# Attention row sums moved into the weighted sums' PSUM bank, with two weighted-sum turns per head instead of three

## The chip, the cores and the metric

The kernel runs on one core of a Trainium2 chip. The metric is the device time in microseconds (us) of one execution; the kernel before takes 891.99 us, the median of three runs from 890.58 to 896.3.

## The reference, cut to what matters

Four batches of eight heads, 1152 keys, 64 dimensions. Neighbouring queries are averaged, so 576 query rows remain per head. The attention output goes through a two-layer network with a parametric ReLU.

```
q_pool = q.reshape(B, H, S // 2, 2, D).mean(axis=3)
scores = scale * (q_pool @ k.T)
attn = exp(scores - max(scores))
attn = attn / (sum(attn) + 1e-09)
x = (attn @ v) laid out as tokens x 512            # 2304 x 512
h = x @ w_in                                       # 512 -> 2048
y = (max(h, 0) + alpha * min(h, 0)) @ w_out        # 2048 -> 512
```

## The kernel before, in words

**Tiling.** A head's scores are computed transposed: nine chunks `c` of 128 keys on the partitions, 576 queries on the free axis in two halves `h` of `HQ` = 288. For each chunk and half two matmuls (L884, L885) fill one of three `s` banks, ScalarE takes the exponential into tile `p` (L897), and `p` (128x2x288) then serves two sums over the keys. The weighted sums `av` = v^T p are matmuls of 64 columns of weights, half 0 into partitions 0-63 and half 1 into 64-127 (L925); the one `av` bank holds 288 of its 512 fp32 columns. The row sums are made in two steps: adds on VectorE (DVE) and GpSimd (POOL) fold three `p` tiles into one partial sum `acc` (L913), and for a pair of heads 12 matmuls with a 128x32 block of ones (L947) sum the partitions of the six partial sums, into an `s` bank, four 32-column groups side by side. ScalarE copies the sums out with eps (L959), a DMA chain through memory turns them for the reciprocal and broadcasts it, and `av` is scaled by it (L984). Matrices of fp32 (not the rounded fp32r) run as two recorded instructions each: 1152 for L925 and 384 for L947.

**Turns.** The scores use the whole 128x128 array, the two sums use it in 64-column or 32-column groups. A run of matmuls in column groups between full-width ones is called a turn here. Before, `G=3` makes three turns of three chunks per head (`weighted`), and one further turn per pair of heads for the row sums (`sums` in `pair_end`).

**Order.** The order of every engine's instructions is worked out by a list scheduler when the kernel is built (`Scheduler`): each task has an engine, a duration, a priority and the buffers it takes, and each engine's queue is in that order on the chip. `prio` is the head's number plus a fraction; `col=True` marks the tasks in column groups and `col_cost` keeps them together. Rings limit the buffers in flight: `PB` for `p`, `AB` for `acc`, one `av` bank.

**Stages.** Up to about 200 us the `m` banks (for the row maxima, L816, reduced by DVE in L833) and three `s` banks hold PSUM, and DVE also converts the first weights. After head 9 (`SWITCH=9`) the banks are dealt anew, one `m` bank pair less, two `h` banks more, and the network's lower part for finished batches (`low_sweep`, L401) fills what TensorE has left. From about 537 us on only the network runs (`low_sweep` of the rest, then `high_sweep`).

Of the kernel before, what the change touches and what calls it, by code (L numbers as in the profile page):

```python
# [182 lines left out]
def attention_ffn(  # L183
# [9 lines left out]
    PB: int = 8,  # L193
# [61 lines left out]
    HQ = SQ // 2  # L255
    NQT = (SQ + P - 1) // P
# [262 lines left out]
    r_rs = Ring([P, HQ], F32, "rs", 1)  # L519
# [13 lines left out]
    s_tasks, acc, avs = {}, {}, {}  # L533
# [338 lines left out]
    def head_main(n, k1, q1, vv):  # L872
        acc[n], avs[n] = [], Buf(r_avs)
        av = Buf(r_av)
        p0, t_acc, t_av, ps_ = None, None, None, []
        for c in range(NC):
# [25 lines left out]
            J = JS[n >= JH]  # L902
            if c % J == 0:

                p0, t_acc = p, None
                part = Buf(r_acc)
                acc[n].append(part)
            else:
                a, b = (p0, p) if c % J == 1 else (part, p)
                eng, dur, e = (DVE, dve(2 * HQ), nc.vector) if c in ADDS[n >= JH] else (POOL, 2.4 * 2 * HQ + 50, nc.gpsimd)  # L910
                t_acc = add(
                    eng, dur,
                    lambda a=a, b=b, part=part, e=e: e.tensor_tensor(out=part.t, in0=a.t, in1=b.t, op=ALU.add),  # L913
                    reads=[a, b], writes=[part], deps=[t_acc] if t_acc else [], prio=n + c / NC, lock=True,
                )

            ps_.append(p)
            if len(ps_) < G and c < NC - 1:
                continue

            def weighted(c=c, ps_=ps_):
                for i, p in enumerate(ps_):
                    e = c - len(ps_) + 1 + i
                    for h in (1, 0):
# [5 lines left out]
            t_av = add(  # L930
                PE, 552 * len(ps_), weighted, reads=[vv] + ps_, writes=[av], deps=[t_av] if t_av else [],
                prio=n + (c + GL) / NC, col=True,
            )
            ps_ = []
# [3 lines left out]
        )  # L938

    def pair_end(n):  # L940
        ps, rs, rsd, rc, rrd = Buf(r_ps), Buf(r_rs), Buf(r_rsd), Buf(r_rc), Buf(r_rrd)

        def sums():
            J = JS[n >= JH]
            for j in range(NC // J):
                for g in (3, 2, 1, 0):
                    nc.tensor.matmul(  # L947
                        out=ps.t[g * 32:(g + 1) * 32, :HQ], lhsT=ones, rhs=acc[n + g // 2][j].t[:, g % 2],
                        start=j == 0, stop=j == NC // J - 1, tile_position=(0, g * 32),
                    )  # L950

        def flat(d):
# [3 lines left out]
        add(PE, 500 * NC // JS[n >= JH], sums, reads=acc[n] + acc[n + 1], writes=[ps], prio=e, col=True, kind="s")  # L956
        add(
            ACT, act(HQ, True) + 93,
            lambda: nc.scalar.activation(out=rs.t, in_=ps.t[:, :HQ], func=AF.Identity, bias=eps),  # L959
            reads=[ps], writes=[rs], prio=e,  # L960
        )
        add(SP, 600, lambda: nc.sync.dma_start(out=rsd.t, in_=rs.t[0:P:32]), reads=[rs], writes=[rsd], prio=e)
# [201 lines left out]
```

## Time and profile before

| | |
|---|---|
| median of three runs | 891.99 us |
| the three runs | 890.58, 891.99, 896.3 us |
| span of the profiled execution, first to last instruction | 894.6 us |
| TensorE busy | 98% of the span |
| DVE, ScalarE, POOL busy | 70%, 58%, 19% |

The profiled execution is another one than the three runs; what lies around its span isn't recorded, and its span lies inside the range of the three. A matmul's recorded duration includes the time it takes to drain, so neighbouring records overlap: what a matmul costs is read from the distance between two starts.

### The profile page before, as it was taken

To read this page: it belongs to the slowest core of one execution; us is meant where nothing else is said; L and a number is where in the kernel's file an instruction comes from. 1 tells how busy PE (TensorE), PEld (TensorE's weight loads), DVE (VectorE), ACT (ScalarE), POOL (GpSimd) and SP (SyncE) were. 2 spreads that over 40 slices of the span, in tenths; PEclk is the share of its full clock that TensorE was granted. 3 is DMA by queue.
4 is the path that set the end of the run, shared out by engine and by line. 5 is a ranking of instruction groups with operands and counts; after the bars stand their busy time and mean duration, and the time that the engine had idled before them with its cause. 6 is when DMAs were issued, how large, how long until landed. Compare 5 with 4: busy or idle time off the path is not lost.

```text
span 894.6 us, 16888 instructions
## 1 busy us (share of the span) xinstructions
PE 874.9 (98%) x6273; PEld 742.6 (83%) x6273; DVE 622.8 (70%) x984; ACT 514.5 (58%) x1337; POOL 171.3 (19%) x126
## 2 busy tenths in 40 slices
PE   8799899999999999999999999999999999999998
PEld 5577666767777787777777779999999999999998
DVE  5899999987877778887798993478953243243332
ACT  4667767676776667766676664466543243333432
POOL 3323322323333323333322320000000000000000
PEclk9999999999999999999999999999999999999999
DMA  8756687677655855954745334955333113112000
GB/s 258 167 146 164 159 209 193 160 206 178 163 123 161 195 158 107 226 127 126 176 107 134 88 101 136 320 176 173 118 106 107 54 54 107 53 54 93 1 27 27
DMA packets 59496, 121.71 MB, mean 136 GB/s; under 512 B 12795, under 2 KB 25622, under 8 KB 59414
## 3 DMA queue, kind: packets, MB, share of 16 engines
q1 hardware_dynamic: 57254, 111.79, 43.8%
q0 software_dynamic: 2160, 8.85, 5.7%
q8 instruction: 49, 0.80, 0.4%
q14 instruction: 33, 0.27, 0.1%
HBM read 92.36 MB, written 19.02 MB: 124 GB/s over the span
## 4 chain that ended last, share of the span: by engine, by line
PE 82%; DVE 12%; ACT 3%; issue 2%; DMA 1%; POOL 0%; DVEq 0%; ACTq 0%; POOLq 0%
PE h L401 30%; PE y L401 16%; PE av L925 12%; PE s L884 7%; PE m L816 7%; PE s L885 6%; DVE bx L833 4%; PE s L947 2%; DVE acc L913 2%; PE av L1048 1%; ACT p L897 1%; PE m L797 1%; DVE q L632 1%; DVE k L619 1%; DVE mm L858 1%
## 5 line engine op out<-in xcount | busy, mean ns | idle before, releaser
L897 ACT ACTIVATE p<-s 128x288 f32<-128x288 f32 x576 | 205.0, 409 | 81.1 <-PE s L885 76.7
L913 POOL TENSOR_TENSOR acc<-acc,p 128x576 f32<-128x576 f32 x96 | 151.1, 1574 | 352.3 <-ACT p L897 159.1
L833 DVE TENSOR_REDUCE bx<-m 128x2 f32<-128x768 f32 x192 | 179.8, 949 | 40.8 <-PE m L816 39.5
L884 PE MATMUL s<-q,k 128*128 128x288 f32 x576 | 171.6, 312 | 1.0 <-ACT p L897 0.8
L885 PE MATMUL s<-q,k 65*128 65x288 f32 x576 | 165.4, 300 | 0.0
L925 PE MATMUL av<-p,vv 128*64 128x288 f32 x1152 | 161.7, 416 | 0.0
L429 DVE SCALAR_TENSOR_TENSOR pos<-neg,nal,pos 128x288 f32<-128x288 f32 x128 | 67.0, 526 | 106.8 <-ACT neg L423 101.9
L884 PEld LDWEIGHTS s<-q,k 128*128 128x128 f32 x576 | 110.4, 192 | 22.4 <-issue 12.0
L418 ACT ACTIVATE pos<-h 128x288 f32<-128x288 f32 x128 | 51.7, 404 | 120.3 <-PE h L401 120.0
L925 PEld LDWEIGHTS av<-p,vv 128*64 128x64 f32 x1152 | 74.5, 137 | 55.6 <-issue 16.7
L401 PE MATMUL h<-x,wh 128*128 128x288 f32 x576 | 117.8, 297 | 0.0
L816 PE MATMUL m<-k,q 128*128 128x384 f32 (+1 forms) x384 | 107.8, 368 | 6.5 <-DVE q L632 3.9
L885 PEld LDWEIGHTS s<-q,k 65*128 65x128 f32 x576 | 110.7, 192 | 0.1
L401 PE MATMUL y<-gs,wh 128*128 128x288 f32 x512 | 103.0, 295 | 0.0
L401 PEld LDWEIGHTS h<-x,wh 128*128 128x128 f32 x576 | 92.4, 188 | 2.9 <-issue 2.7
L435 ACT ACTIVATE gs<-pos 128x288 fp32r<-128x288 f32 x128 | 56.7, 444 | 60.8 <-DVE pos L429 60.3
L440 DVE TENSOR_TENSOR gs<-pos,gs 128x288 fp32r<-128x288 f32 x128 | 59.1, 464 | 45.5 <-ACT gs L435 45.1
L816 PEld LDWEIGHTS m<-k,q 128*128 128x128 f32 (+1 forms) x384 | 63.2, 198 | 27.7 <-issue 11.8
L401 PE MATMUL h<-x,wl 128*128 128x288 f32 x288 | 84.8, 294 | 0.0
L401 PEld LDWEIGHTS y<-gs,wh 128*128 128x128 f32 x512 | 82.1, 188 | 0.0
L913 DVE TENSOR_TENSOR acc<-p 128x576 f32<-128x576 f32 x96 | 72.4, 755 | 10.8 <-ACT p L897 9.6
L401 PE MATMUL y<-gs,wl 128*128 128x288 f32 x256 | 75.4, 294 | 0.0
(97 smaller groups left out, 1269.4 us busy)
## 6 DMA issues: line engine op xcount, KB each, us to landing
kk<-kt SPq DMA_DIRECT2D x63, 288.0 KB
wraw<-wt SPq DMA_DIRECT2D x32, 512.0 KB
x<-xs SPq DMA_DIRECT2D x48, 288.0 KB
qs<-qt SPq DMA_DIRECT2D x16, 576.0 KB
vv<-vt SPq DMA_DIRECT2D x32, 288.0 KB
xs<-x SPq DMA_DIRECT2D x64, 144.0 KB
k<-k SPq DMA_DIRECT2D x62, 144.0 KB
qs<-qt POOLq DMA_DIRECT2D x15, 576.0 KB, 7.0
```

The lines of the kernel that those rows point to most:

```text
L401: nc.tensor.matmul(out=ps[:, :HQ], lhsT=w[a, c // DMO][:, c % DMO:c % DMO + P], rhs=lo(hl), start=(first and i == 0), stop=(last and i == 2),)
L418: ACT, act(HQ, True), lambda: nc.scalar.activation(out=pos.t, in_=ps.t[:, :HQ], func=AF.Relu),
L429: lambda: nc.vector.scalar_tensor_tensor(out=pos.t, in0=neg.t, scalar=nal[:, f:f + 1], in1=ps.t[:, :HQ] if NT else pos.t, op0=ALU.mult, op ...
L435: ACT, act(HQ), lambda: nc.scalar.activation(out=gs.t[:, 0], in_=pos.t, func=AF.Copy),
L440: lambda: nc.vector.tensor_tensor(out=gs.t[:, 1], in0=pos.t, in1=gs.t[:, 0].bitcast(F32), op=ALU.subtract),
L816: nc.tensor.matmul(out=ms.t[:, i, :JW], lhsT=q1.t[d, PAD + t * P:PAD + (t + 1) * P], rhs=k1.t[d, j * JW:(j + 1) * JW], start=True, stop=True,)
L833: lambda c=c, e=e, step=step, m=len(pair), ms=ms: nc.vector.tensor_reduce(out=bx.t.rearrange("p t j -> p (t j)")[:, c:e + 1:step], in_=ms. ...
L884: nc.tensor.matmul(out=ps.t[:, :HQ], lhsT=k1.t[:, s], rhs=q1.t[:, q], start=True, stop=False)
L885: nc.tensor.matmul(out=ps.t[:, :HQ], lhsT=k2[n % 2][:, s], rhs=q2[n % 2][:, PAD + q.start:PAD + q.stop], start=False, stop=True)
L897: lambda ps=ps, p=p, h=h: nc.scalar.activation(out=p.t[:, h], in_=ps.t[:, :HQ], func=AF.Exp, scale=SCALE),
L913: lambda a=a, b=b, part=part, e=e: e.tensor_tensor(out=part.t, in0=a.t, in1=b.t, op=ALU.add),
L925: nc.tensor.matmul(out=av.t[h * D:(h + 1) * D, :HQ], lhsT=vv.t[:, e], rhs=p.t[:, h], start=(e == 0), stop=(e == NC - 1),)
```

## The change

Weighted sums come in two turns per head, chunks 0-3 and 4-8 (`GROUPS`). Partial sums come from `PARTS`: heads 0-11 have four (chunks 0-3, 4-6, 7, 8; the last two are the `p` tiles themselves), heads 12-31 have three (0-4, 5-7, 8). Adds per head: five (DVE 1 and 5, POOL 2, 3 and 6) or six (DVE 1, 6 and 7, POOL 2, 3 and 4), before six (DVE 1, 4, 7, POOL 2, 5, 8). Each partial sum, seen as 576 columns, is cut into four quarters of `SW` = 144, and four matmuls with the block of ones put their sums into columns 288-431 of the `av` bank (`total`), with a priority right behind the second group. `pair_end` no longer has a turn of its own; ScalarE copies the sums per head, and two DMAs instead of one bring a pair's sums to memory. `PB` goes from 8 to 11, `AB` from 7 to 4, and the `rs` ring from one tile of 288 columns to two of 144.

```
-    PB: int = 8,
+    PB: int = 11,
...
-    G: int = 3,
-    JS: tuple = (3, 9),
-    JH: int = 32,
-    AB: int = 7,
-    ADDS: tuple = ((1, 4, 7), (1, 4, 7)),
+    GROUPS: tuple = (3, 8),
+    PARTS: tuple = (((0, 1, 2, 3), (4, 5, 6), (7,), (8,)), ((0, 1, 2, 3, 4), (5, 6, 7), (8,))),
+    JH: int = 12,
+    AB: int = 4,
+    ADDS: tuple = ((1, 5), (1, 6, 7)),
...
+    SW = SQ // 4
...
-    r_rs = Ring([P, HQ], F32, "rs", 1)
+    r_rs = Ring([P, SW], F32, "rs", 2)
...
+            if c in heads:
+
+                part, first, t_acc = p, True, None
             else:
...
+                a, part = part, Buf(r_acc) if first else part
...
-            if len(ps_) < G and c < NC - 1:
-                continue
...
+            if c in GROUPS:
...
+                t_av.append(add(
+                    PE, 552 * len(ps_), weighted, reads=[vv] + ps_, writes=[av], deps=t_av[-1:],
+                    prio=n + (c + GL) / NC, col=True,
+                ))
+                ps_ = []
+            if c in tails:
+
+                def total(part=part):
+                    q = part.t.rearrange("p h q -> p (h q)")
+                    for g in (3, 2, 1, 0):
                         nc.tensor.matmul(
-                            out=av.t[h * D:(h + 1) * D, :HQ], lhsT=vv.t[:, e], rhs=p.t[:, h],
-                            start=(e == 0), stop=(e == NC - 1),
+                            out=av.t[g * 32:(g + 1) * 32, HQ:HQ + SW], lhsT=ones, rhs=q[:, g * SW:(g + 1) * SW],
+                            start=False, stop=True, tile_position=(0, g * 32), skip_group_check=True,
                         )
...
+                totals.append((total, part, n + (max(c, GROUPS[1]) + GL) / NC + 0.001))
+        for total, part, p in totals:
+            add(PE, 245, total, reads=[part], writes=[av], deps=t_av[:1], prio=p, col=True)
...
+        add(
+            ACT, act(SW, True) + 93,
+            lambda: nc.scalar.activation(out=sums[n].t, in_=av.t[:, HQ:HQ + SW], func=AF.Identity, bias=eps),
+            reads=[av], writes=[sums[n]], prio=n + 1,
+        )
...
-        def sums():
-            J = JS[n >= JH]
-            for j in range(NC // J):
-                for g in (3, 2, 1, 0):
-                    nc.tensor.matmul(
-                        out=ps.t[g * 32:(g + 1) * 32, :HQ], lhsT=ones, rhs=acc[n + g // 2][j].t[:, g % 2],
-                        start=j == 0, stop=j == NC // J - 1, tile_position=(0, g * 32),
-                    )
...
-        add(PE, 500 * NC // JS[n >= JH], sums, reads=acc[n] + acc[n + 1], writes=[ps], prio=e, col=True, kind="s")
...
-        add(SP, 600, lambda: nc.sync.dma_start(out=rsd.t, in_=rs.t[0:P:32]), reads=[rs], writes=[rsd], prio=e)
+        for i in range(2):
+            add(
+                SP, 600,
+                lambda i=i: nc.sync.dma_start(
+                    out=rsd.t[2 * i:2 * i + 2].rearrange("g q -> (g q)").rearrange("(a b) -> a b", b=SW),
+                    in_=sums[n + i].t[0:P:32],
+                ),
+                reads=[sums[n + i]], writes=[rsd], prio=e,
+            )
```

## Rows read from the trace of the kernel before

**Rows 1.** The page: span, and the clock granted to TensorE in 40 slices.
```profile
span 894.6 us, 16888 instructions
...
PEclk9999999999999999999999999999999999999999
```

**Rows 2.** By stage: stretch, length, busy us (xcount) of PE, PEld, DVE, ACT, POOL.
```profile
60.00:200.00 140.00, 134.14 (x925) 94.58 (x925) 134.16 (x196) 102.82 (x266) 44.33 (x32) 0.99 0.72 187
200.00:537.00 337.00, 335.29 (x2459) 258.54 (x2457) 278.36 (x390) 230.20 (x611) 107.70 (x71) 1.00 0.57 144
537.00:895.00 358.00, 353.72 (x2671) 353.25 (x2667) 165.77 (x338) 148.57 (x386) 0.00 (x0) 1.00 0.31 100
```

**Rows 3.** The chain that ended last, 60-200 us: shares of that stretch by line.
```profile
by line: DVE bx L833 16.1%; DVE acc L913 8.2%; PE av L925 7.4%; issue 7.4%; PE s L884 5.8%; ACT p L897 5.3%; PE m L816 4.7%; PE s L885 4.2%; ACT k L605 3.7%; DVE k L619 3.4%; DMA q<-mm 3.3%; DVE wmag L359 3.2%; DVE q L632 3.1%; DVE wl L323 
```

**Rows 4.** Waits in 200-537 us, weight loads, then DVE: total us, times, longest us.
```profile
PEld m L816 <- DVE bx L833: 4.3, 6, 1.3
...
DVE bx L833 <- PE m L816: 32.4, 45, 1.7
```

**Rows 5.** Timeline of TensorE around one weighted turn: start us, us, line.
```profile
201.56 0.30 PE L884 MATMUL s<-q,k 128*128 128x288 f32 x1
201.69 0.30 PE L885 MATMUL s<-q,k 65*128 65x288 f32 x1
201.92 1.68 PE L925 MATMUL av<-p,vv 128*64 128x288 f32 x12
203.53 0.40 PE L884 MATMUL s<-q,k 128*128 128x288 f32 x1
203.76 0.29 PE L885 MATMUL s<-q,k 65*128 65x288 f32 x1
```

**Rows 6.** Timeline of TensorE in four 10 ns stretches inside turns: start us, us.
```profile
202.46 0.41 PE L925 MATMUL av<-p,vv 128*64 128x288 f32 x2
...
203.19 0.41 PE L925 MATMUL av<-p,vv 128*64 128x288 f32 x2
...
212.29 0.43 PE L947 MATMUL s<-acc,ones 128*32 128x288 f32 x4
...
212.53 0.43 PE L947 MATMUL s<-acc,ones 128*32 128x288 f32 x4
```

**Rows 7.** Timeline of TensorE: a turn with weighted sums and row sums joined.
```profile
210.18 1.68 PE L925 MATMUL av<-p,vv 128*64 128x288 f32 x12
211.78 1.66 PE L947 MATMUL s<-acc,ones 128*32 128x288 f32 x24
213.37 0.40 PE L884 MATMUL s<-q,k 128*128 128x288 f32 x1
```

**Rows 8.** Stretches with L925 alone, then those with tile `acc` alone (columns of rows 2).
```profile
28.00:200.00 172.00, 56.08 (x396) 25.82 (x396) 0.97 0.69 176
200.00:537.00 337.00, 105.59 (x756) 48.63 (x756) 1.00 0.57 144
...
28.00:60.00 32.00, 0.00 (x0) 0.00 (x0) 4.40 (x6) 9.22 (x6) 0.89 0.54 126
60.00:200.00 140.00, 8.31 (x120) 3.52 (x120) 20.20 (x27) 40.96 (x28) 0.99 0.72 187
200.00:537.00 337.00, 18.25 (x264) 7.45 (x264) 47.76 (x63) 100.96 (x63) 1.00 0.57 144
```

**Rows 9.** Timeline of TensorE: four matmuls of 384 columns, and the next start.
```profile
204.43 0.87 PE L816 MATMUL m<-k,q 128*128 128x384 f32 x4
205.14 0.30 PE L884 MATMUL s<-q,k 128*128 128x288 f32 x1
```

**Rows 10.** 40 ns with L947 alone: TensorE busy (xcount), weight loads busy (xcount).
```profile
211.77:211.81 0.04, 0.03 (x4) 0.03 (x5) 1.00 0.57 115
```

**Rows 11.** ScalarE groups: busy us, mean ns of one | idle before.
```profile
L853 ACT ACTIVATE mm<-s 5x128 fp32r<-5x128 f32 x31 | 8.1, 262 | 12.8 <-PE s L849 12.7
...
L959 ACT ACTIVATE rs<-s,eps 128x288 f32<-128x288 f32 x16 | 8.0, 499 | 12.7 <-PE s L947 12.7
```

**Rows 12.** Timeline: the last attention output is stored; the first matmul that needs it.
```profile
557.88 2.91 SPq L1006 DMA_DIRECT2D xs<-x  x4
...
579.11 0.29 PE L401 MATMUL h<-x,wh 128*128 128x288 f32 x1
```

More of the change, by code (lines that the diff above doesn't have):

```diff
@@ L532, in attention_ffn @@
     q2_b = [Buf() for n in range(NH)]
-    s_tasks, acc, avs = {}, {}, {}
+    s_tasks, sums, avs = {}, {}, {}
     def old_users(n):
@@ L872, in head_main @@
     def head_main(n, k1, q1, vv):
-        acc[n], avs[n] = [], Buf(r_avs)
+        avs[n], sums[n] = Buf(r_avs), Buf(r_rs)
         av = Buf(r_av)
-        p0, t_acc, t_av, ps_ = None, None, None, []
+        t_acc, t_av, ps_, totals = None, [], [], []
+        late_head = n >= JH
+        heads, tails = [g[0] for g in PARTS[late_head]], [g[-1] for g in PARTS[late_head]]
         for c in range(NC):
@@ L901, in head_main @@
                 )
-            J = JS[n >= JH]
[L903 to L907, printed above, removed]
-            else:
-                a, b = (p0, p) if c % J == 1 else (part, p)
-                eng, dur, e = (DVE, dve(2 * HQ), nc.vector) if c in ADDS[n >= JH] else (POOL, 2.4 * 2 * HQ + 50, nc.gpsimd)
+            if c in heads:
+                part, first, t_acc = p, True, None
+            else:
+                a, part = part, Buf(r_acc) if first else part
+                eng, dur, e = (DVE, dve(2 * HQ), nc.vector) if c in ADDS[late_head] else (POOL, 2.4 * 2 * HQ + 50, nc.gpsimd)
@@ L911, in head_main @@
                 t_acc = add(
                     eng, dur,
-                    lambda a=a, b=b, part=part, e=e: e.tensor_tensor(out=part.t, in0=a.t, in1=b.t, op=ALU.add),
-                    reads=[a, b], writes=[part], deps=[t_acc] if t_acc else [], prio=n + c / NC, lock=True,
+                    lambda a=a, b=p, part=part, e=e: e.tensor_tensor(out=part.t, in0=a.t, in1=b.t, op=ALU.add),
+                    reads=[a, p], writes=[part], deps=[t_acc] if t_acc else [], prio=n + c / NC, lock=True,
@@ L915, in head_main, with weighted @@
                 )
+                first = False
             ps_.append(p)
-            if len(ps_) < G and c < NC - 1:
-                continue
[L921 to L924, printed above, removed]
+            if c in GROUPS:
+                def weighted(c=c, ps_=ps_):
+                    for i, p in enumerate(ps_):
+                        e = c - len(ps_) + 1 + i
+                        for h in (1, 0):
+                            nc.tensor.matmul(
+                                out=av.t[h * D:(h + 1) * D, :HQ], lhsT=vv.t[:, e], rhs=p.t[:, h],
+                                start=(e == 0), stop=(e == NC - 1), skip_group_check=True,
+                            )
[4 more added lines that the diff above has]
+                ps_ = []
@@ L925, in weighted @@
+            if c in tails:
+                def total(part=part):
+                    q = part.t.rearrange("p h q -> p (h q)")
+                    for g in (3, 2, 1, 0):
                         nc.tensor.matmul(
-                            out=av.t[h * D:(h + 1) * D, :HQ], lhsT=vv.t[:, e], rhs=p.t[:, h],
-                            start=(e == 0), stop=(e == NC - 1),
-                        )
-            t_av = add(
-                PE, 552 * len(ps_), weighted, reads=[vv] + ps_, writes=[av], deps=[t_av] if t_av else [],
-                prio=n + (c + GL) / NC, col=True,
-            )
@@ L938, in head_main @@
         )
-    def pair_end(n):
-        ps, rs, rsd, rc, rrd = Buf(r_ps), Buf(r_rs), Buf(r_rsd), Buf(r_rc), Buf(r_rrd)
-        def sums():
-            J = JS[n >= JH]
-            for j in range(NC // J):
-                for g in (3, 2, 1, 0):
-                    nc.tensor.matmul(
-                        out=ps.t[g * 32:(g + 1) * 32, :HQ], lhsT=ones, rhs=acc[n + g // 2][j].t[:, g % 2],
-                        start=j == 0, stop=j == NC // J - 1, tile_position=(0, g * 32),
-                    )
+        add(
[3 more added lines that the diff above has]
+        )
+    def pair_end(n):
+        rsd, rc, rrd = Buf(r_rsd), Buf(r_rc), Buf(r_rrd)
         def flat(d):
@@ L955, in pair_end @@
         e = n + E0
-        add(PE, 500 * NC // JS[n >= JH], sums, reads=acc[n] + acc[n + 1], writes=[ps], prio=e, col=True, kind="s")
[L957 to L961, printed above, removed]
-        add(SP, 600, lambda: nc.sync.dma_start(out=rsd.t, in_=rs.t[0:P:32]), reads=[rs], writes=[rsd], prio=e)
+        for i in range(2):
[6 more added lines that the diff above has]
+                reads=[sums[n + i]], writes=[rsd], prio=e,
+            )
         add(SP, 600, lambda: nc.sync.dma_start(out=rc.t, in_=flat(rsd.t)), reads=[rsd], writes=[rc], prio=e)
```

1 line of the change is left out of this document (removed).

## The prediction

> **What bounds the kernel now.** I read the stages first, then the chain and the waits of each stage, and at last single turns of TensorE. The stages [rows 2]: from 537 us on TensorE is busy 353.72 of 358 us, with nothing of this change in it, so that stretch keeps its length. In 200-537 us TensorE is busy 335.29 of 337 us, while DVE has 278.36 and ScalarE 230.20; the weight loads waited for DVE only 4.3 us in all [rows 4]. There time is TensorE time: what it no longer does is taken over by the network's matmuls that otherwise wait for the stretch after 537 us. In 60-200 us there is no such filler yet, and TensorE (134.14) and DVE (134.16 of 140 us) are both nearly full. The chain there changes engines all the time: DVE's reduce is its largest share, DVE's adds have 8.2%, TensorE's weighted sums 7.4% [rows 3]. So a saving on one engine counts there in part. The granted clock is in its top tenth in every slice [rows 1], the 2.4 GHz level in both stretches (0.99 and 1.00 [rows 2]); the change leaves TensorE no emptier, so I expect nothing of the clock.
>
> **What a turn costs.** Two full-width score matmuls start 0.13 us apart (201.56, 201.69). The weighted turn starts 0.23 after the second, the next full-width matmul starts 1.61 after that, and its follower 0.23 later [rows 5]. Inside the turn a pair (both halves) starts every (203.19 - 202.46) / 3 = 0.243 us [rows 6], so the six pairs of three chunks are 1.46 us of columns, 0.485 per chunk. What is left is the price of the turn: 1.61 - 1.46 = 0.15 inside, 0.10 ahead of it and 0.10 behind it, together 0.35 us. A joined turn lasts 213.37 - 210.18 = 3.19 us [rows 7]; its row sums are six steps of four at 0.24 [rows 6], 1.45 us, so 3.19 - 1.46 - 1.45 - 0.15 = 0.13 us is the change from 64-column to 32-column groups.
>
> **What a new row sum costs.** No row shows four 144-column matmuls in column groups. In the full-width rows the time goes with the columns: 384 of them take (205.14 - 204.43) / 4 = 0.178 us [rows 9] and 288 take 0.13 [rows 5], 1.37 times as long for 1.33 times the columns, so next to nothing is fixed. Halved, a step of four is 0.12 us and a partial sum (two steps) 0.245. The other bound is that the instructions set the pace and not the columns: then a step of four costs what it does now, 0.485 per partial sum. I take 0.245, because four matmuls and five weight loads stand inside 40 ns at the start of a row-sum turn [rows 10], far above the pace that the upper bound needs. A rule speaks against this, in the Trainium skill, TensorE: Matmul & The Clock Gate, Back-to-back issue gap: a stream of weight load and matmul pairs settles at about 81 ns per matmul of 128 columns. By that, eight matmuls are 0.65 us per partial sum and, as an estimate, the whole sum below becomes a loss of 32 us. The trace disagrees: it already runs pairs of 288 columns at 61 ns (four in 0.243 [rows 6]).
>
> **TensorE from 200 us on.** The stretch holds 756 / 12 = 63 weighted turns, which is 21 heads of three, and 264 / 24 = 11 row-sum groups [rows 8]. Two of these follow a weighted turn directly (the one at 210.18 is shown [rows 7]), nine stand alone: 72 turns and two joints. After, 21 heads make 42 turns with 21 joints. Turns: -30 x 0.35 = -10.5 us. Joints: +19 x 0.13 = +2.5. Columns: 11 x 1.45 = 16.0 before; after, 20 heads of three partial sums and one of four, 64 x 0.245 = 15.7: -0.3. Sum -8.3 us. The weighted columns stay.
>
> **TensorE before 200 us.** 396 / 12 = 33 weighted turns and 120 / 24 = 5 row-sum groups, one of them joined: 37 turns. After, 11 heads make 22 turns and 11 joints: -15 x 0.35 + 10 x 0.13 = -4.0 us. Columns: 44 partial sums x 0.245 = 10.8 against 5 x 1.45 = 7.3: +3.5. So TensorE gains only 0.5 us here, and I count it as nothing.
>
> **DVE before 200 us.** 33 adds, three per head, took 4.40 + 20.20 = 24.6 us [rows 8]; 11 go, 8.2 us. How much of it counts: the chain spends 8.2% of 140 us = 11.5 us in these adds [rows 3] out of 20.20 busy, 57%. So -4.7 us. The bounds are 0 (TensorE, busy as long as DVE, ends just as late) and -8.2. The POOL keeps three adds per head, so what DVE loses to it stays.
>
> **What is added.** ScalarE copies 32 sums of 144 columns in place of 16 of 288. A copy of 128 columns took 262 ns and one of 288 with eps 499 [rows 11]; between them, 0.28 to 0.5, I take 0.3: 9.6 us in place of 8.0, beside other work, since ScalarE has 107 us free in 200-537 and 37 in 60-200 [rows 2]. If that cover were gone it would cost 1.6 us, at the upper bound 8. The copy holds the single `av` bank 0.3 us longer; the next user is the next head's first turn, whose priority stands four chunks later, so nobody waits. The copy of the weighted sums now also waits for the row sums behind them, 3 x 0.245 + 0.13 = 0.9 us, with the same cover. The `s` bank that a pair's row sums took, and which held back the scores, comes free: a gain that I leave out. SyncE issues 16 DMAs more, 4.5 KB per pair as before; the second waits for the second head's sums, and behind it queue the loads of heads to come, issued a head or more early. The end is covered too: the last attention output is stored at 557.88-560.8 and first used at 579.11 [rows 12], 18 us of cover. What goes out in smaller parts leaves the wait for both heads as it was. Buffers: three `p` tiles more, three `acc` fewer, and the five-chunk group with its lag of 3.5 chunks holds 8.5 of 11 tiles, before 6.5 of 8.
>
> **The longer turn.** This is the added wait. The second turn grows from 1.61 to 10 x 0.243 + 0.15 + 0.13 + 3 x 0.245 = 3.4 us, during which no score and no row maximum is made. Queued behind it are the score matmuls, and ScalarE's exponentials and DVE's reduce wait for these. DVE now waits 32.4 us for the maxima in 200-537, at most 1.7 at once, about one turn [rows 4]. If the long turn adds 1.8 us of DVE wait per head, that is 21 x 1.8 = 38 us; DVE has 337 - 278 = 59 us of idle time, of which these waits are a part, and TensorE has the network's work meanwhile. Bounds: 0, and at worst all 38 us less the 59 - 32 = 27 us that DVE has idle otherwise, 11 us. As TensorE's own waits for DVE were 4.3 us in 74 turns, I take a third of them more, +1.5 us.
>
> **Sum.** -8.3 - 4.7 + 1.5 = -11.5 us. Against its own time, the span of 894.6 us, that is 883.1. The span lies 2.6 us over the median 891.99, inside the range of the three runs; what lies around it isn't recorded. From the median: 880.5 us, -1.3%.
>
> **The rivals.** (1) Early relief off the path, and a dearer long turn: TensorE's 134.14 us of 140 speak for it, the 57% of adds on the chain against it. The early term is 0 and the waits cost 4 us: 891.99 - 8.3 + 4 = 887.7. (2) The change doesn't do what it says: where the scheduler has a partial sum ready too late (the last DVE add comes one chunk before the group ends), the row sums stand in a turn of their own. For it: 13 of 16 stand alone now. Against it: the lag of 3.5 chunks, and their priority just behind the group. Price 0.35 - 0.13 = 0.22 us x 32 heads = +7: 887.5. (3) Slower: the pace of the instructions sets the row sums. 32 heads have 12 x 4 + 20 x 3 = 108 partial sums; at 0.485 they cost 108 x 0.24 = +25.9: 906. From 108 x 0.11 us more, a partial sum of 0.35 us, the whole gain is lost. [Rows 10] speak against it. The pace that the Trainium skill states, named above, would lie behind this rival, further out. (4) Slower: the long turn starves DVE and ScalarE and the planner doesn't refill them. At 0.36 us lost per head and turn (11.5 / 32) the gain is gone; at 1 us per head it is 891.99 - 13 + 32 = 911. For it speaks the single `m` bank pair after the switch, against it the idle time of both engines and the filler.
>
> **How the numbers follow.** Forecast 0.58, rival 1 0.17, rival 2 0.11, rival 3 0.06, rival 4 0.08. A measurement of this kernel tells about 1% from no change, 8.9 us: faster means under 883, which is the forecast, 0.58. Same is rivals 1 and 2, 0.28. Slower is rivals 3 and 4, 0.14. The likeliest case alone reaches from 874 (the early term at -8.2, no added waits, the `s` bank's part) to 885. The range has to take in the cases within 1% and the bound of 11 us on the waits: 891.99 - 8.3 - 4.7 + 11 = 890, and a little of rival 4: 873 to 894.
>
> **What would show it.** Right: 64 turns with 16 and 20 weighted records by turns (four per chunk), and row-sum records right behind the longer ones; distances of 0.12 us between steps of the row sums; the stretch from the first network matmul to the end of attention about 8 us shorter in sum; fewer DVE adds (84 in place of 96) and the first network matmul some 5 us earlier. Wrong: row sums in turns of their own (rival 2); steps over 0.17 us (rival 3); TensorE's idle time before L884 or L816 in 200-537 grown by more than 4 us, with DVE's wait for `m` over 70 us (rivals 1 and 4); the first network matmul no earlier (rival 1).

## The result, and the profile after

The changed kernel takes 897.95 us (median), the kernel before 890.58 in the same comparison: ratio 1.0088, 95% interval 1.0065 to 1.011. The prediction was 880.5 us, range 873 to 894: wrong in sign and outside the range.

The page of the profile of the changed kernel; the last line is TensorE's granted clock by slices (as [rows 1]):

```profile
span 896.1 us, 17842 instructions
...
PE 875.4 (98%) x6753; PEld 749.6 (84%) x6753; DVE 614.4 (69%) x972; ACT 515.3 (58%) x1353; POOL 161.4 (18%) x126
...
PEclk9899999999999999999999999999999999999999
```

Its stages (columns: stretch, then length, busy time and records of TensorE, its weight loads, DVE, ScalarE and POOL, then granted clock, DMA share, GB/s), to set beside [rows 2]:

```profile
60.00:200.00 140.00, 137.67 (x1132) 99.08 (x1129) 128.22 (x185) 102.02 (x270) 46.31 (x34) 1.00 0.73 190
200.00:537.00 337.00, 332.01 (x2631) 259.43 (x2627) 269.21 (x378) 225.56 (x604) 94.03 (x67) 1.00 0.56 142
537.00:895.00 358.00, 353.42 (x2660) 352.89 (x2660) 167.43 (x343) 148.11 (x386) 0.00 (x0) 0.99 0.30 98
```

The shape is that of before: TensorE nearly full everywhere. So I counted. A head ends with ScalarE's copy of its weighted sums, one record per head; the starts of the 3rd, 12th and last of these copies split the run. The kernel before was profiled a second time (e9 below, span 888.0), and its late part repeats to 0.1 us: 319.6 us from the 12th copy to the last in the first trace, 319.7 in the second.

| us | before, first trace | before, second trace | after |
|---|---|---|---|
| start to 3rd copy | 76.2 | 73.5 | 70.4 |
| 3rd to 12th copy | 136.8 | 132.7 | 133.3 |
| 12th to last copy | 319.6 | 319.7 | 334.8 |
| last copy to the end | 362.0 | 362.1 | 357.6 |

The loss is in the last 20 heads and what follows: 334.8 + 357.6 = 692.4 against 681.8, +10.6 us, where I had forecast -8.3 + 1.5 = -6.8. The start isn't the kernel's: a kernel with the changed one's very order (e15) had its 3rd copy at 74.4, and one with the instructions of before (e18) at 70.0.

The next table takes that late stretch apart, from the starts of TensorE's records. "Full" is the full-width work at 0.133 us for 288 columns and 0.175 for 384; turns cost 0.345 us and joints 0.13, the prediction's prices; "rest" is what is left. The weighted columns are 87.3 us in every kernel. (A joint is a change between 64-column and 32-column groups inside a turn, either way.)

| 12th to last copy | length | full | turns, joints | their cost | row-sum columns | rest | then to the end |
|---|---|---|---|---|---|---|---|
| before, second trace | 319.7 | 190.3 | 69, 1 | 23.9 | 13.2 | 4.8 | 362.1 |
| after | 334.8 | 194.8 | 77, 5 | 27.2 | 14.6 | 10.3 | 357.6 |
| e16, sums in the second turn | 333.4 | 194.7 | 40, 20 | 16.4 | 14.6 | 17.5 | 358.4 |
| e17, sums in the next head | 344.0 | 214.7 | 40, 20 | 16.4 | 14.9 | 8.8 | 357.6 |
| e8, joined at the head's end | 351.3 | 227.1 | 40, 20 | 16.4 | 14.6 | 5.7 | 352.7 |
| e14, first six heads only | 332.3 | 193.2 | 67, 2 | 23.4 | 13.1 | 14.9 | 359.5 |
| e13, first twelve heads only | 319.2 | 189.9 | 68, 1 | 23.6 | 13.1 | 5.1 | 361.7 |

(Lengths are between copies, the shares between TensorE's first and last record in them; they differ by up to 3 us.)

**Turns.** The whole kernel has 131 turns and 11 joints where the prediction had 64 and 32. 67 turns are row sums alone, 45 of them of a single partial sum; 40 of the 67 stand ahead of their head's second group, 27 behind it. Over the whole kernel turns and joints cost 46.6 us in place of 38.0, and the row-sum columns 108 x 0.245 = 26.5 in place of 16 x 1.45 = 23.2: +11.9, where the span grew by 8.1 (896.1 against 888.0) and the start alone is 3.1 shorter. Timeline of the changed kernel (start us, us, line):

```profile
514.92 0.29 PE L402 MATMUL h<-x,wl 128*128 128x288 f32 x1
515.15 0.45 PE L940 MATMUL av<-acc,ones 128*32 128x144 f32 x8
515.53 0.33 PE L850 MATMUL s<-identr,mx 128*128 128x128 f32 x1
515.79 2.65 PE L925 MATMUL av<-p,vv 128*64 128x288 f32 x20
518.37 0.45 PE L940 MATMUL av<-p,ones 128*32 128x144 f32 x8
518.63 0.43 PE L940 MATMUL av<-acc,ones 128*32 128x144 f32 x8
```

One partial sum goes ahead of the second group, one full-width matmul before it, and pays for a turn of its own: 515.53 - 515.15 = 0.38 us, 0.245 of it columns, with 0.10 on either side. In the code a `total` waits for the first group alone (`deps=t_av[:1]`), and its priority near n + 1.3 is far ahead of the network's 1000, so the scheduler places it in the first gap after its partial sum is ready.

**The seam.** At the end of attention TensorE waits, and then runs slowly. Timeline of the changed kernel, with the wait in brackets, and its granted clock in the stretch behind it (columns as above, TensorE and weight loads first):

```profile
535.35 0.43 PE L940 MATMUL av<-p,ones 128*32 128x144 f32 x8
537.82 0.45 PE L940 MATMUL av<-acc,ones 128*32 128x144 f32 x8 [2.04 <-DVE acc L913]
539.26 0.84 PE L402 MATMUL h<-x,wh 128*128 128x288 f32 x2 [0.99 <-ACT rs L954]
```

```profile
539.00:543.20 4.20, 3.94 (x18) 3.94 (x19) 2.38 (x6) 1.91 (x6) 0.00 (x0) 0.59 0.03 4
543.20:544.00 0.80, 0.80 (x8) 0.80 (x8) 0.00 (x0) 0.00 (x0) 0.00 (x0) 1.00 0.00 0
```

2.04 us for the last head's add, 0.99 for the copy of its row sums, then 4.2 us at a granted clock of 0.59, mostly the 1.2 GHz level, after which it is 1.00 again. By slices of 20 us, the clock granted less than full costs 1.8 us here after 60 us; in the second trace of before it costs nothing, and no matmul waits for another engine between 510 and 660 us.

So the late +10.2 us are +14.7 in the stretch between records and -4.5 after it. In the stretch 4.5 are full-width work, which is as much less behind it; turns are +3.3, the rest +5.5, and row-sum columns +1.4, which the kernel before has behind its last copy, as the sums of its last pair. The seam makes some 5.2 us of the loss: waits of 2.04 and of 0.4 us for another, and, mostly behind the last copy at 538.5, the 0.99 and the clock's 1.8. About 2 us are in short waits between 250 and 500 us: five of 0.3 to 1.1 us beyond the prices make 3.9, where the kernel before has three, 1.9.

### The profile page after: what moved, and what is told of

Read it like the earlier page. It is cut to its first block, busy times and chain, and to the rows that moved or that the text cites. A ratio compares the mean times of both kernels' runs of the same rounds, so it can differ in the third digit from the quotient of the medians.

```text
span 896.1 us, 17842 instructions
## 1 busy us (share of the span) xinstructions
PE 875.4 (98%) x6753; PEld 749.6 (84%) x6753; DVE 614.4 (69%) x972; ACT 515.3 (58%) x1353; POOL 161.4 (18%) x126
## 4 chain that ended last, share of the span: by engine, by line
PE 86%; DVE 7%; DMA 3%; ACT 1%; issue 1%; SPq 1%; POOL 0%; DVEq 0%; ACTq 0%; POOLq 0%
PE h L402 29%; PE y L402 16%; PE av L925 14%; PE s L887 8%; PE m L817 8%; PE s L888 7%; PE av L940 3%; DMA r<-rrd 2%; DVE bx L834 1%; PE m L798 1%; DVE r L995 1%; DVE k L620 1%; DVE x L1007 1%; DVE acc L913 1%; DVE wbits L348 1%
## 5 line engine op out<-in xcount | busy, mean ns | idle before, releaser
L900 ACT ACTIVATE p<-s 128x288 f32<-128x288 f32 x576 | 202.1, 410 | 75.5 <-PE s L888 70.2
L913 POOL TENSOR_TENSOR acc<-acc,p 128x576 f32<-128x576 f32 x96 | 141.2, 1471 | 349.5 <-DVE acc L913 161.9
L925 PE MATMUL av<-p,vv 128*64 128x288 f32 x1152 | 153.8, 412 | 0.0
L430 DVE SCALAR_TENSOR_TENSOR pos<-neg,nal,pos 128x288 f32<-128x288 f32 x128 | 70.0, 550 | 111.2 <-ACT neg L424 106.5
L887 PEld LDWEIGHTS s<-q,k 128*128 128x128 f32 x576 | 109.9, 191 | 21.9 <-ACT p L900 13.5
L925 PEld LDWEIGHTS av<-p,vv 128*64 128x64 f32 x1152 | 77.1, 137 | 56.5 <-issue 10.2
L817 PE MATMUL m<-k,q 128*128 128x384 f32 (+1 forms) x384 | 104.2, 358 | 1.8 <-DVE q L633 1.2
L402 PE MATMUL h<-gs,wh 128*128 128x288 f32 x320 | 66.8, 301 | 0.0
```

The costliest lines, as they stand in the source:

```text
L402: nc.tensor.matmul(out=ps[:, :HQ], lhsT=w[a, c // DMO][:, c % DMO:c % DMO + P], rhs=lo(hl), start=(first and i == 0), stop=(last and i == 2),)
L430: lambda: nc.vector.scalar_tensor_tensor(out=pos.t, in0=neg.t, scalar=nal[:, f:f + 1], in1=ps.t[:, :HQ] if NT else pos.t, op0=ALU.mult, op ...
L817: nc.tensor.matmul(out=ms.t[:, i, :JW], lhsT=q1.t[d, PAD + t * P:PAD + (t + 1) * P], rhs=k1.t[d, j * JW:(j + 1) * JW], start=True, stop=True,)
L887: nc.tensor.matmul(out=ps.t[:, :HQ], lhsT=k1.t[:, s], rhs=q1.t[:, q], start=True, stop=False)
L900: lambda ps=ps, p=p, h=h: nc.scalar.activation(out=p.t[:, h], in_=ps.t[:, :HQ], func=AF.Exp, scale=SCALE),
L913: lambda a=a, b=p, part=part, e=e: e.tensor_tensor(out=part.t, in0=a.t, in1=b.t, op=ALU.add),
```

## The experiments

All ratios are to the kernel before, run beside them; e9 is one run of the kernel before, 889.78 us.

| run | median us | ratio and 95% interval |
|---|---|---|
| e1 joined, strict guard | 915.91 | 1.029, 1.0245 to 1.0334 |
| e2 the guard alone | 907.35 | 1.0196, 1.0157 to 1.0235 |
| e3 two groups alone, guard | 921.62 | 1.0349, 1.0302 to 1.0396 |
| e4 e1 without four early partial sums | 930.14 | 1.0453, 1.0401 to 1.0505 |
| e5 dearer change of shape | 903.16 | 1.0128, 1.0081 to 1.0175 |
| e6 three groups, joined | 894.69 | 1.0046, 1.0018 to 1.0074 |
| e7 three groups, own turns | 908.76 | 1.0203, 1.0151 to 1.0254 |
| e8 joined, light guard | 908.65 | 1.0192, 1.0156 to 1.0229 |
| e10 later conversions | 894.17 | 1.0061, 1.0032 to 1.0089 |
| e11 e6 and e10 | 893.82 | 1.005, 1.0023 to 1.0078 |
| e12 e6 without four early partial sums | 907.71 | 1.02, 1.0152 to 1.0247 |
| e13 first twelve heads only | 887.51 | 0.9977, 0.9945 to 1.0009 |
| e14 first six heads only | 899.63 | 1.0097, 1.0062 to 1.0131 |
| e15 sums once per head, same order | 900.17 | 1.0113, 1.0059 to 1.0167 |
| e16 sums in the second turn, same order | 898.52 | 1.0109, 1.0063 to 1.0155 |
| e17 sums in the next head's turn | 907.59 | 1.0212, 1.0164 to 1.026 |
| e18 order alone | 891.75 | 1.0028, 1.0007 to 1.0049 |

### Joining the row sums (e1, e2, e8, e6, e7, e5)

e1 makes the row sums part of the second group's task. The scheduler then finds no order unless a high sweep of the network waits for the sweep before it; e2 is the changed kernel with that guard alone, and e8 is e1 with a lighter one (a sweep may run five hidden blocks ahead).

```
-            add(PE, 245, total, reads=[part], writes=[av], deps=t_av[:1], prio=p, col=True)
+        add(PE, 552 * len(ps_) + 245 * len(totals), both, reads=[vv] + ps_ + parts, writes=[av], ...)
```

> The changed kernel with one edit in the attention: a head's row sums are issued by the same task as its second group of weighted sums, so they can't stand in a turn of their own. (A second edit, also in the other kernels of this set, keeps the matmuls of one high sweep behind the hidden layer of the sweep before; without it the scheduler finds no order to the end.) The built order then has 64 turns, 32 of them joined; the changed kernel has 131 with 11 joints. Theory A, the turns cost the time: 131 x 0.345 + 11 x 0.13 = 46.6 us becomes 64 x 0.345 + 32 x 0.13 = 26.2, so 20 us less than the changed kernel's 898: 874 to 882, 1% or more under the kernel before. Theory B, the longer stretch without scores starves ScalarE and DVE, whatever the number of turns: TensorE's time outside matmuls and turns after 204 us grows from 10 us to over 20, and the time stays at 890 or above.

> The changed kernel with only the edit that keeps the high sweeps apart; the order before the last stage is the same to the last instruction. All theories: as the changed kernel, 898 us within 3, 1.0088 of the kernel before within 0.003. If it differs by more, what the other kernels of this set show is in part this edit's.

> The joined kernel of the first set (two groups, row sums with the second, 64 turns) with a lighter edit in the last stage: a high sweep may be five hidden blocks ahead of the sweep before's end instead of none. Theory A: 20 us less than the changed kernel's 898, 878. Theory P: the last copy to avs stays near 554, TensorE still idles some 14 us for the last batch's x before 580; only the 10 us that the stricter edit cost come back: 903 to 908.

The guard costs 9.4 us (907.35 - 897.95), against what was expected of it; TensorE's rest between 640 and 680 us, which is nothing in the changed kernel, is 10 us in e2. Joining gives the 64 turns and 32 joints, 20.4 us less than the changed kernel's 131 and 11, and is slower than its control even so. In e8 the 11 us that the late turns save (27.2 to 16.4) go to the network: full-width work in the stretch rises from 194.8 to 227.1, the last copy comes at 554.1, and TensorE then waits for the last batch's input, until 576.8 (540 to 600 us; total us, times, longest):

```profile
PE h L402 <- DMA xh<-xs: 13.7, 1, 13.7
```

The prediction's "18 us of cover" at the end was used up.

e6 joins at three groups, which needs no guard; e7 leaves the row sums in turns of their own there.

```
-    GROUPS: tuple = (3, 8),
+    GROUPS: tuple = (2, 5, 8),
```

> The changed kernel with three weighted groups of three chunks, as before the change, and a head's row sums issued with its third group; the four early partial sums and the av bank for the sums stay. 96 turns and 32 joints: 96 x 0.345 + 32 x 0.13 = 37.3 us of turns. Theory A: 9 us less than the changed kernel, 889. Theory P: the longest stretch falls from 3.5 to 2.6 us, so more than that is won: the last copy to avs comes at 530 or earlier and the time is 880 to 887.

> The changed kernel with three weighted groups of three chunks and row sums placed by the scheduler as in the change: 156 turns, 25 joints, 57.1 us of turns and the shortest stretches of all. Theory A: 10 us more than the changed kernel, 908. Theory P: the short stretches make up for them, 898 or less, with the last copy to avs at 535 or earlier.

e7 comes out as theory A had it, e6 as neither theory. e7 against e6 has 60 more turns and 7 fewer joints, 19.8 us, and is 14 us slower: this agrees with turns that count when they come on top, though the order differs too. But e6 against e8 has 32 more turns, 11 us, and is 14 us faster; 9 of the 14 are e8's rest between 640 and 680 us, where its guard acts, and that leaves 5. So the count of turns doesn't order these kernels.

e5 only makes a change of shape dearer for the scheduler (`COL` to 1.0), which groups more: 100 turns, 42 joints, 6.6 us less turn cost, and 5.2 us slower, with its last copy at 546.2.

> The changed kernel with one constant of the scheduler: the price in priority of going into or out of column groups is 1.0 instead of 0.099. The order has 100 turns and 42 joints (131 and 11). Theory A, turns alone: 100 x 0.345 + 42 x 0.13 = 40.0 us in place of 46.6, 7 us less than the changed kernel: 889 to 893. Theory P, the pace: what counts is how long TensorE makes no scores at a stretch, since that delays the end of the attention; joined stretches are longer, so no gain, 896 or more, and the last copy to avs (538.5 us in the changed kernel, 532.6 before) comes later, after 541.

### Parts of the change alone (e3, e4, e12, e13, e14)

e3 is the kernel before with two groups per head and nothing else (`PB` 9, `AB` 6, strict guard).

> The kernel before with two weighted groups (chunks 0-3 and 4-8) in place of three and nothing else of the change: row sums per pair in an s bank, three partial sums per head, nine p tiles and six acc tiles, and the high sweeps kept apart. The order has 72 turns and 8 joints, before 109 and 3. Theory A: 109 x 0.345 + 3 x 0.13 = 38.0 us becomes 72 x 0.345 + 8 x 0.13 = 25.9, so 12 us less than before: 877 to 881. Theory B: no better than before, 888 or above, with DVE's wait for the row maxima over 50 us in the stretch after 200 us (32 before).

Slower by 3.5%, with turn cost 25.9 in place of 38.0 us. The guard has its share, 18 us of rest between 640 and 680; 15 us between 520 and 600 lie outside it. DVE's wait for the maxima is 36.4 us and not over 50, so theory B has the time right and its sign wrong.

e4 and e12 take the four early partial sums back (`JH` = 0) from e1 and e6.

> As the joined kernel, but all heads have the three partial sums of the late ones: 96 adds on DVE in place of 84, 96 partial sums in place of 108. Theory C, the early heads end with DVE: 12 adds of 0.75 us come back, at least 57% of them on the chain, +5 us, and the row sums give back 12 x 0.245 = 3 us where TensorE ends last: 2 to 6 us slower than the joined kernel. Theory D, TensorE ends the early heads as often: as fast as the joined kernel or up to 3 us faster. The end of head 11's weighted sums (copy to avs) tells them apart: some 5 us later than in the joined kernel under C, the same under D.

> Three groups with the row sums joined to the third, and all heads with the three partial sums of the late ones: no early heads with four, 96 adds on DVE in place of 84. With two groups the same step cost 14 us. Theory C, the early heads end with DVE: the twelfth copy to avs, at 200.2 us with the four, comes at 207 or later, and the time is 8 us or more over 894.7. Theory D, TensorE ends them as often: within 2 us of 200 and 890 to 895, since 12 partial sums of 0.245 us are saved.

They are worth 13 to 14 us where row sums belong to a head: heads 3 to 12 take 142.0 us in e12 and 130.0 in e6. But the kernel before needs 132.7 and the changed one 133.3. So the early sums mostly pay for what the own row sums cost there, more than theory C had forecast for e4 (2 to 6 us).

e13 and e14 keep the late heads as before (three groups, pair sums) and change only heads 0 to 11, or 0 to 5: four partial sums, put into the weighted bank in the third group's turn.

```
+                if early and c == NC - 1:
+                    for part in acc[n]:
+                        # four 144-column matmuls into av.t[:, HQ:HQ + SW], as in total
```

> The kernel before, with only heads 0 to 11 changed: four partial sums of their own each, put into the weighted sums' bank in the turn of the third group. Heads 12 to 31 keep three groups and pair sums as before. If the early relief is a gain by itself: the 12th copy of the weighted sums at 200 to 204 us against 206.2, the stretch from there to the last copy 320 us as before, and so 881 to 885 us, 0.6 to 1.1% under the kernel before. If the relief only moves the wait, or if row sums in that bank slow a head whatever the turns: 889 us or more.

> The same for heads 0 to 5 alone. If the early relief is a gain by itself that goes with the number of heads: half of it, 885 to 888 us, with the 12th copy near 204 us. If only the very first heads matter (the idle time of TensorE lies mostly before 100 us): as fast as with twelve. If the relief only moves the wait: 890 us.

e13 is the fastest kernel here, but its interval includes 1, and its time lies between its two expectations; early heads gain 132.7 - 132.2 = 0.5 us, its late part is that of before to 0.5 us. e14 is the surprise and misses all three: its late heads are those of before too, and their stretch is 12.6 us longer. In that stretch only the order differs. Its timeline and granted clock at the seam:

```profile
519.98 0.40 PE L891 MATMUL s<-q,k 65*128 65x288 f32 x1 [0.86 <-DMA q<-mm]
...
523.06 0.61 PE L890 MATMUL s<-q,k 128*128 128x288 f32 x1 [2.15 <-ACT p L903]
523.47 0.44 PE L891 MATMUL s<-q,k 65*128 65x288 f32 x1
523.71 0.44 PE L890 MATMUL s<-q,k 128*128 128x288 f32 x1
```

```profile
523.00:528.00 5.00, 4.94 (x20) 3.91 (x22) 4.77 (x7) 3.97 (x11) 1.70 (x1) 0.50 0.47 150
```

After the 2.15 us wait the same matmuls start 0.24 us apart in place of 0.13: granted clock 0.50, the 1.2 GHz level, for 5 us. Its rest is 10.1 us over before; waits of 0.9, 2.1 and 2.5 us account for half of it, and the clock for a part of the other half: 5.2 us are lost in 520 to 560, some of them while TensorE waits or behind the last copy at 538.1. A loss of this size can thus come without any of the new row sums in the stretch.

### The changed kernel's order, with other row sums (e15, e16)

These keep the changed kernel's order of every engine and move only which matmuls are emitted where.

```
+                    if c == GROUPS[1]:           # e16: in the second turn, from that group's last p tile
+                        for k in range(len(totals)):
+                            # four 144-column matmuls, in place of total(), which emits nothing
```

> The changed kernel with its order kept instruction for instruction; only the row sums are emitted once per head, at the place of the head's last partial sum, as many columns as before but all from that partial sum (so the row sums of the other parts are left out and the result is not the reference's). Turns 131 and 11 joints become 90 and 6: 46.6 to 31.8 us of turn cost, 14.8 less. If the turns are the loss: 883 us, against 897.95. If what counts is when a head's last sum is ready, or the waits at the end of attention: 893 us or more.

> The changed kernel with its order kept instruction for instruction; the row sums' columns stand in the turn of the second group and read that group's last chunk in place of the partial sums (so the row sums are those of the wrong tile and the result is not the reference's). That is the order of work that the forecast assumed: 64 turns and 32 joints, 26.2 us in place of 46.6, and no wait for the adds. If only the count of turns failed in the forecast: 877 to 881 us. If the longer turn of 3.4 us starves DVE and ScalarE, or the order itself is slow: 890 us or more, with TensorE's idle time in 200 to 540 us above 25 us.

e16 has the 64 turns and 32 joints of the forecast, and the turn the predicted length (timeline; 336.53 - 333.08 = 3.45 us, forecast 3.4):

```profile
333.08 2.65 PE L925 MATMUL av<-p,vv 128*64 128x288 f32 x20
335.65 0.94 PE L933 MATMUL av<-p,ones 128*32 128x144 f32 x24
336.53 0.62 PE L817 MATMUL m<-k,q 128*128 128x384 f32 x2
```

Yet its time is that of the changed kernel. The late stretch from copy to copy:

```profile
205.70:539.10 333.40, 325.87 (x2607) 260.00 (x2605) 266.18 (x376) 221.03 (x601) 94.30 (x67) 1.00 0.56 143
```

Turn cost falls by 10.8 us there, the rest rises by 7.2, and 2.2 more pass between TensorE's last record and the last copy; the stretch is 1.4 shorter. With an order that is fixed, the relief of TensorE turns into waiting. Before 200 us it is the same: turn cost 9.4 in place of 19.1, rest 32.5 in place of 21.0. e15 says the same with 90 turns. This was the decisive pair: the surplus turns exist and have their price, but at this order they are not what the time follows.

e16 also says what the seam waits for. Its last row sums need no add and are done by 536.6, and still TensorE waits, longer than in the changed kernel (TensorE, then ScalarE, then DVE):

```profile
535.61 0.94 PE L933 MATMUL av<-p,ones 128*32 128x144 f32 x24
539.80 0.85 PE L402 MATMUL h<-x,wh 128*128 128x288 f32 x2 [3.25 <-ACT rs L957]
...
538.76 0.41 ACT L419 ACTIVATE pos<-h 128x288 f32<-128x288 f32 x1 [1.86 <-DVE gs L441]
539.07 0.40 ACT L952 ACTIVATE avs<-av 128x288 f32<-128x288 f32 x1
539.36 0.39 ACT L957 ACTIVATE rs<-av,eps 128x144 f32<-128x144 f32 x1
...
536.94 0.69 DVE L324 TENSOR_TENSOR k<-wmag,k 128x512 fp32r<-128x512 f32 x1
537.55 0.75 DVE L913 TENSOR_TENSOR acc<-acc,p 128x576 f32<-128x576 f32 x1
538.22 0.82 DVE L441 TENSOR_TENSOR gs<-pos,gs 128x288 fp32r<-128x288 f32 x2
```

In the code the network's four last `h` banks are opened once all users of attention's banks are done, the two last copies among them. ScalarE has these behind a `pos` that waits for DVE's `gs`, and DVE has that behind the last weight conversions and the last adds. So at the seam it is the order of DVE's and ScalarE's queues that holds TensorE, also where the row sums need no add.

### Row sums one head later (e17)

The row sums of a head stand in the first turn of the next, where they are always ready (`deps` on its partial sums, a guard of eight hidden blocks).

> The changed kernel with each head's row sums in the first turn of the next head, in that head's bank, where all partial sums have long been ready; the pair's end comes one head later. High sweeps start at most eight hidden blocks before the previous sweep's end, without which the scheduler finds no order. 64 turns, 32 joints, 26.2 us of turn cost, and no closing copy waits for an add. If joined turns pay once they need not wait: 879 to 885 us. If the longer stretches delay attention's end as they did in the other joined kernels: last copy of the weighted sums at 545 us or later and 895 us or more.

Here the scheduler is free to use the relief, and does: 214.7 us of full-width work in the late stretch, rest 8.8. But a head now takes 344.0 / 20 = 17.2 us, before 16.0. DVE's waits for the maxima in 200 to 540 us, of the changed kernel, e16 and e17, then TensorE's waits in e17 in 526 to 900 (total us, times, longest):

```profile
DVE bx L834 <- PE m L817: 33.7, 45, 1.5
...
DVE bx L834 <- PE m L817: 34.9, 44, 1.5
...
DVE bx L839 <- PE m L822: 41.1, 43, 3.4
```

```profile
PE h L402 <- DMA xh<-xs: 6.4, 1, 6.4
PE y L402 <- ACT gs L436: 3.7, 3, 1.9
```

In e17 DVE waits up to 3.4 us for maxima, about a joined turn (2.96 us here), against 1.7 in [rows 4]: rival 4's mechanism. A long turn alone doesn't make it, since e16 has one of 3.45 us and waits at most 1.5. And the last copy comes at 544.9, so that the network runs out of finished inputs: 24 us of waits and lost clock after 520, some 6.5 of them at the guard. Less all of these the span of 902.5 would be 878 us, as an estimate, near the forecast; no run shows such a kernel.

### The seam and the order (e9, e10, e11, e18)

e10 is the changed kernel with `RP` from 31.0 to 31.8, which moves the last weight conversions off DVE's final heads; e11 does the same to e6.

> The changed kernel with one constant moved: the six weight conversions that reuse the attention's buffers have priority 31.8 instead of 31.0, behind the last head's last two adds. In the changed kernel the last row sums wait 2.0 us for such an add, ScalarE's copy behind it holds the network 1.0 us more, and the granted clock is 0.57 in the 4 us after. Theory T, this tail is part of the loss: no wait over 0.5 us for the add at the end, no dip of the clock, 3 to 5 us less than the changed kernel: 893 to 895. Rival: the conversions end later in exchange and the network waits for them instead: 897 or more.

> Three groups with the row sums joined to the third (894.7 us in the set before), and the conversions' priority at 31.8: 3 to 5 us less by theory T, 890 to 892, as fast as the kernel before; 894 or more by the rival.

The stretch from 536 to 543 us of the kernel before (second trace), the changed kernel and e10 (columns as above):

```profile
536.00:543.00 7.00, 7.00 (x55) 7.00 (x54) 0.22 (x1) 2.09 (x6) 0.00 (x0) 1.00 0.34 108
...
536.00:543.00 7.00, 4.19 (x24) 3.90 (x25) 5.35 (x12) 3.06 (x9) 0.00 (x0) 0.76 0.30 103
...
536.00:543.00 7.00, 6.20 (x64) 5.78 (x63) 5.35 (x11) 3.55 (x10) 0.00 (x0) 1.00 0.44 159
```

In e10 the wait for the add is gone, the granted clock is 1.00 there, and the time is 894.17: 3.8 us less than the changed kernel, as theory T had it. The two ratios' intervals overlap; of the two traces, e10's is 4.4 us shorter from the 12th copy to the end. e11 shows no gain over e6; it has a 2.0 us wait for the copy of the row sums in its place, so it decides nothing.

e9 is the kernel before profiled again. e18 is the kernel before with one figure of the scheduler, `552 * len(ps_)` to `520 * len(ps_)`: same instructions, another order.

> The kernel before once more, for a second profile: the first one's span, 894.6 us, is longer than what its other runs suggest (median 890.6). If the difference lies in the start, as I think, the first three heads end earlier (third copy to avs at 76.2 us in the first profile, then at 70 to 74) and the span is 886 to 891; the stretch from the twelfth copy to avs to the last (319.6 us) is the same within 1 us.

> The kernel before with one figure of the scheduler changed and no instruction: it takes a weighted chunk for 520 ns in place of 552, which with its prices for entering and leaving column groups makes a turn of 1.81 us, as measured. Same instructions, another order, 108 turns and 4 joints in place of 109 and 3. If the late loss of the changed kernel is that of a new order as such: 896 to 901 us, with last copy of the weighted sums at 532 us or later and 5 us or more of idle TensorE in 520 to 560. If the order is worth little and the row sums make the loss: 888 to 892 us, last copy at 525 to 528 us.

e18 meets its second expectation: 891.75 us, 1.2 slower than before, with the last copy at 525.6; its late stretch is 323.1, its rest 1.9 over before, with 2.1 us of waits and 1.8 of clock in 520 to 560. That doesn't show that the row sums make the loss, as the expectation has it: e14 loses 9 us with late heads that have none of the new ones. So what an order costs by itself is between a little (e18) and about 1% (e14). At the seam the order holds TensorE also without the row sums' need for an add (e16), and e10 wins back some 4 of its 5 us by moving conversions; how much of the remaining late loss belongs to the row sums and how much to the order that the scheduler made for them stays open.

## Why the prediction was wrong, point by point

- **What a turn and a row sum cost** was right. A lone partial sum takes 0.38 us inside and the long turn 3.45; six steps of four 144-column matmuls stand in 336.53 - 335.65 = 0.88 us; less the turn's 0.15 that is 0.12 a step, as forecast. Rival 3 is out. The rule that spoke for it, in the Trainium skill, TensorE: Matmul & The Clock Gate, Back-to-back issue gap, would give 1.9 us for these 24 records, as an estimate from its 81 ns; the trace decides against it for 32-column matmuls.
- **"21 heads make 42 turns with 21 joints"** was the first failed step. The 20 late heads have 77 turns with 5 joints. Rival 2 had row sums in turns of their own, but as sums that come too late, and priced at one turn per head; there are about two (67 in 32 heads), and 40 of the 67 stand ahead of the second group, where being early and not being late parts them. I read the priority and not the `deps`.
- **"There time is TensorE time"** was the second, and the deeper one. 335.29 of 337 us busy [rows 2] was read as: what TensorE no longer does shortens the stretch. e16 takes 10.8 us of turns out and gets 1.4; e17 and e8 fill the relief with the network, and attention ends later. The network only fills, so a full TensorE is no proof. At the seam DVE's and ScalarE's queues hold the end of attention; what holds the single head before it stays open.
- **DVE's early relief, -4.7 us**: adds in heads 3 to 12 fell by 20.3 - 13.5 = 6.8 us as forecast (second trace; [rows 8] has 20.20 in the first), the time by nothing (132.7 to 133.3; 132.2 in e13). Taken apart as above, these heads have 4.9 us less rest and 4.4 more turns, 1.3 more columns: what was freed went into the row sums' own turns, which the forecast didn't have. DVE also lost time elsewhere (next section). Rival 1 had the size of this term.
- **The longer turn, +1.5 us**: DVE's wait for `m` stayed at 33.7 us in 204 to 539 [rows 4: 32.4], while the row sums mostly weren't in that turn. Where they are it is 34.9 at the same order (e16), and 41.1 (e17) and 48.6 (e1) where the scheduler made another. So the length of the turn alone doesn't cost it.
- **"18 us of cover" at the end** holds in the changed kernel and fails where attention ends 19 us later or more (e17, e8). **"Nothing of the clock"** failed: 1.8 us at the seam, after the waits there, which the forecast didn't have.

## What to carry to other kernels

A filled engine shows that work was found for it, not that it sets the time; ask what ends the stage if that engine gets faster, and test it by taking the work out at an unchanged order. Where a scheduler writes the order, read what each new task waits for as well as its priority, and count the turns in the built order before pricing them. Look at the seam between stages first: here waits of 3.0 us cost 1.8 us more in granted clock.

## What the hardware showed that was not expected

**The clock after short waits.** Behind waits of 0.86 and 2.15 us in e14 the granted clock was 0.50, the 1.2 GHz level, over 5 us, and behind waits of 2.04 and 0.99 us in the changed kernel 0.59 over 4.2 us. In e18 it fell behind waits of 0.9 and 1.2 us (0.91 in the slice from 520 to 540); the changed kernel's single waits of up to 1.0 us between 250 and 500 us cost nothing of the clock. By 20 us slices after 60 us, the granted clock lost nothing in the second trace of before, e13 and e10, 1.8 us in the changed kernel, 3.6 in e18, 7.0 in e14 and 12 in e8: in these it goes with the waits.

**DVE beside POOL.** DVE's smallest operation grew. Groups of DVE, 3rd to 12th copy (busy us, mean ns | idle before), of the kernel before, second trace, then of the changed kernel:

```profile
L913 DVE TENSOR_TENSOR acc<-p 128x576 f32<-128x576 f32 x27 | 20.3, 750 | 7.6 <-ACT p L897 7.3
...
L858 DVE TENSOR_TENSOR mm<-mm 1x64 fp32r<-1x64 f32 x9 | 1.8, 200 | 0.5 <-ACT mm L853 0.5
```

```profile
L913 DVE TENSOR_TENSOR acc<-p 128x576 f32<-128x576 f32 x18 | 13.5, 750 | 3.6 <-ACT p L900 3.4
L324 DVE TENSOR_TENSOR wl<-wmag,wh 128x512 fp32r<-128x512 f32 x8 | 7.0, 879 | 0.9 <-ACT wh L321 0.8
...
L859 DVE TENSOR_TENSOR mm<-mm 1x64 fp32r<-1x64 f32 x9 | 4.3, 475 | 2.5 <-ACT mm L854 2.4
```

Timeline of the changed kernel, DVE and POOL:

```profile
89.84 1.41 POOL L913 TENSOR_TENSOR acc<-acc,p 128x576 f32<-128x576 f32 x1
...
90.52 0.80 DVE L859 TENSOR_TENSOR mm<-mm 1x64 fp32r<-1x64 f32 x1
```

Five of the nine meet a POOL add and end 0.07 us after it (90.52 + 0.80 = 91.32, the add ends at 91.25); the other four take 0.2 us, as the nine do before, none of which meets a POOL add. The Trainium skill, SBUF — State Buffer, SBUF: two separate sides, says why: a DVE operation with two inputs in SBUF and a GpSimd operation that reads SBUF take one port pair in turn, each for its whole length. The trace agrees. With `wl` (681 to 879 ns in the two traces) it is 4 us of the 6.8 that the removed adds freed; seven `wmag` operations (840 to 692 ns) give 1 back.
